# Attention and two feed-forward layers on one core: dividing P by its row sums before the transpose, V for two heads in one stationary block, and x by way of DRAM

## The chip, the cores and the metric

The kernel runs on one core of a Trainium2 chip. The metric is the device time of one execution in microseconds (us). Its engines, by the names in the profile: PE (TensorE matmuls) and PEld (TensorE weight loads), DVE (VectorE), ACT (ScalarE), POOL (GpSimd), SP (SyncE, which here only issues DMAs).

## The reference, cut to what matters

```python
q, k, v: (4, 8, 576, 64) float32          # batch, heads, tokens, head width
def _attn_ref(q, k, v, tau):
    scores = matmul(q, k.T) / sqrt(64)
    scores = where(scores >= max(scores) - tau, scores, -1e9)
    attn = exp(scores - max(scores))
    attn = attn / (sum(attn) + 1e-9)
    return matmul(attn, v)
def _moe_ref(x, w_in, w_out, g_ln):       # 2304 tokens, 512 -> 1024 -> 512
    h = x @ w_in
    solu = h * softmax(h)
    return (layer_norm(solu) * g_ln) @ w_out
def _moe2_ref(x, w_in, w_out):            # 512 -> 2048 -> 512
    h = x @ w_in
    return (h * tanh(softplus(h))) @ w_out
```

The output is _moe2_ref(_moe_ref(attention)). The weights of the two feed-forward layers (first FFN and second FFN below) arrive as float64 and are turned into float32 in the kernel.

## The kernel before

**Attention.** The 32 heads are handled as 16 pairs. For each pair, nine score tiles of 128 x 576 are made: for each of four row tiles of 128 queries one per head, and one tile that holds the last 64 queries of both heads (`s_tile`, L484). A score tile is q as stationary operand in two float32r halves (Qhh, Qb), k as moving operand (Kst), 288 columns at a time (L501). DVE takes the row maximum (L507), makes from it a bias and a threshold in one small instruction on two columns (L508), ACT computes the exponential into the SBUF tile e (L509), DVE sets to zero what lies under the threshold (L511). `turn` (L527) transposes e on PE against the identity, in blocks of 128, into the PSUM tile tp (L536, L539), and `leave` (L517) copies tp into ex, ey or er: every fourth copy on DVE (L522), the others on ACT (L523). `pv` (L562) multiplies V with the transposed tile, for each head in two pieces of 256 and 320 query columns (L575). These matmuls are float32, and the stationary block of 128 columns holds 64 columns of V and 64 of ones, so that half of the PSUM tile acc holds the product and the other half the row sums, 64 times.

**Division and x.** ACT copies the product into xT, which stays in SBUF, and the row sums into ss (L588, L589). `norm` (L595) transposes ss on DVE in 32 x 32 blocks (L598), adds 1e-9 (L600), takes the reciprocal (L601), transposes back (L602), and POOL multiplies x by it (L603). `x_split` (L614) splits x for 128 tokens into two float32r halves XH and XL on ACT and POOL.

**First FFN.** Per 128 tokens: `moe_h` (L641) makes two tiles mo of 512 columns, `layer_norm` normalizes, `moe_t` transposes (L689) and splits (L694, L696), and `moe_y` (L710) makes the output for 256 tokens in the PSUM tile smt; `moe_y` writes its two halves to DRAM. Tiles of a batch can start when its four pairs are done.

**Second FFN.** It reads these halves back and works in units of 256 or 512 tokens (L877, L903). Its buffers take the place of the attention's buffers (`opens`, L758), so it starts when the attention is over.

**Weights.** `convert` (L392) turns 128 x 256 float64 words into float32: two instructions on ACT (L404, L410), three on DVE (L412, L413, L415), one on POOL (L417).

**PSUM.** Eight banks: two score tiles st of two banks each, one each for tp, acc, mo and smt.

**What sets the order.** Every piece of work is a task with an engine, a modelled duration and its dependencies. `Plan` (L49) lists tasks with priorities from a backward pass, tries several weights, keeps the shortest list, and writes the program in that order; each engine then runs its own list strictly in that order, SP its DMA issues too. A slot of a buffer is handed on when all tasks that used it are done (L199 to L205).

Of the kernel before, what the change touches and what calls it, by code (L numbers as in the profile page):

```python
# [227 lines left out]
def kernel(  # L228
# [35 lines left out]
    NV = 2  # L264
    DV = 4
# [36 lines left out]
    w2o = [dram.tile([FG * 128, DM], F32, name=f"w2o{i}") for i in range(NG)]  # L302
    part = [dram.tile([DM, PN], F32, name=f"part{i}") for i in range(U0)]
# [158 lines left out]
    count, EXS = [0], []

    def load_v(p):

        v = VH[p % NV]
        war = [t for h in range(2) for c in range(2) for t in PVT[p - NV, h, c]] if p >= NV else []
        ld = [add("SP", dma(128 * KT * 256), lambda a=a: D(f(main(v)[:, :, 2 * a]), v2[p // (H_ // 2), p % (H_ // 2), :, a].rearrange(
            "p (k d) -> p k d", d=64)), war) for a in range(2)]
        ld.append(add("SP", dma(128 * 512), lambda: D(f(last(v)[:, 0:4:3]), v4[p // (H_ // 2), p % (H_ // 2)].rearrange("p (a d) -> p a d", d=64)), war))  # L470
        VL[p] = v, ld
# [522 lines left out]
```

## Time and profile before

| | |
|---|---|
| median of 3 runs | 1025.27 us (1023.78 to 1025.28) |
| the profiled execution | 1024.83 us; its span in the trace 1023.0 us |
| PE busy | 971.9 us (95%) |
| DVE busy | 625.7 us (61%) |
| ACT busy | 581.1 us (57%) |
| POOL busy | 302.3 us (30%) |
| chain that ended last | PE 70%, DVE 8%, ACT 7% |

A share of busy time is a mean over the whole span. The work has stretches with different limits, so the table by stretch in the rows below tells more: attention and the conversion of weights at first, then attention together with the first FFN of finished batches, then the rest of the first FFN and the second FFN. A mean duration of an instruction is from its start to its end; the next one on the same engine can start before that end.

### The profile page before, as it was taken

The numbers are of one execution on the slowest core, as the hardware profiler recorded it, in microseconds if no ns is written. First come the engines' busy times: TensorE is split into PE (matmuls) and PEld (weight loads), VectorE is DVE, ScalarE is ACT, GpSimd is POOL, SyncE is SP. The second block draws the span as 40 slices with busy tenths as digits, with TensorE's granted clock in tenths as the row PEclk, the third lists the DMA queues.
The fourth block names the chain that finished last, engine by engine and source line by source line (L and its number), as shares of the span: only waits on it lengthen the run. The fifth ranks groups of instructions, "written<-read, shape, count | busy, mean of one in ns | idle before, by whom it ended". The sixth has DMA issues, their size and how long they took to land.

```text
span 1023.0 us, 15619 instructions
## 1 busy us (share of the span) xinstructions
PE 971.9 (95%) x5648; PEld 836.8 (82%) x5648; DVE 625.7 (61%) x1309; ACT 581.1 (57%) x1166; POOL 302.3 (30%) x309
## 2 busy tenths in 40 slices
PE   3788889999999999999989999999999999999998
PEld 2676677878888898888869999998888888888887
DVE  6789989989878878778684333234544445322222
ACT  5688778988776957777674555343544234312220
POOL 3344555364432332242232110023333223200000
PEclk9799899999999999999999999999999999999999
DMA  5233324232233232231234312398645434313312
GB/s 167 75 99 93 113 70 114 69 98 91 79 99 105 75 90 68 76 93 55 68 107 141 103 44 88 107 324 283 196 138 164 152 124 144 127 59 104 124 51 72
DMA packets 106013, 113.81 MB, mean 111 GB/s; under 512 B 27472, under 2 KB 82384, under 8 KB 105936
## 3 DMA queue, kind: packets, MB, share of 16 engines
q1 hardware_dynamic: 105792, 112.82, 35.3%
q8 instruction: 44, 0.72, 0.3%
q14 instruction: 33, 0.27, 0.1%
q10 hardware_dynamic: 144, 0.00, 0.0%
HBM read 93.39 MB, written 19.40 MB: 110 GB/s over the span
## 4 chain that ended last, share of the span: by engine, by line
PE 70%; DVE 8%; ACT 7%; issue 1%; DMA 1%; ACTq 0%; SPq 0%
PE o L903 14%; PE h L877 13%; PE smt L710 8%; PE acc L575 8%; PE h2b L877 7%; PE mo L641 6%; PE o2b L903 5%; PE st L501 4%; PE tp L536 3%; ACT e L509 2%; DVE e L511 2%; DVE m L507 1%; PE mo L689 1%; DVE m L508 1%; DMA cr<-w_out 1%
## 5 line engine op out<-in xcount | busy, mean ns | idle before, releaser
L509 ACT ACTIVATE e<-st,m,sc 128x576 f32<-128x576 f32 x144 | 118.5, 830 | 41.6 <-DVE m L508 34.1
L511 DVE SCALAR_TENSOR_TENSOR e<-st,m,e 128x576 f32<-128x576 f32 x144 | 116.1, 813 | 35.5 <-ACT e L509 34.8
L417 POOL TENSOR_TENSOR cf<-cf,cl 128x256 uint32<-128x256 uint32 x96 | 71.7, 752 | 204.5 <-DVE cf L415 165.2
L501 PE MATMUL st<-Kst,Qhh 128*128 128x288 f32 (+2 forms) x352 | 111.4, 337 | 17.7 <-DVE e L511 7.6
L507 DVE TENSOR_REDUCE m<-st 128x1 f32<-128x576 f32 x144 | 107.5, 751 | 21.3 <-PE st L501 20.7
L536 PE MATMUL tp<-ident,e 128*128 128x128 f32 x576 | 92.1, 284 | 14.7 <-DVE e L511 8.6
L501 PE MATMUL st<-Kst,Qb 128*128 128x288 f32 (+2 forms) x352 | 97.8, 302 | 0.0
L536 PEld LDWEIGHTS tp<-ident,e 128*128 128x128 f32 x576 | 70.0, 145 | 32.2 <-DVE e L511 8.9
L710 PE MATMUL smt<-LH,W2H 128*128 128x256 f32 x288 | 90.9, 316 | 2.5 <-DVE yl L721 2.4
L501 PEld LDWEIGHTS st<-Kst,Qhh 128*128 128x128 f32 x352 | 70.4, 200 | 25.1 <-DVE Kst L479 7.3
L710 PE MATMUL smt<-LL,W2H 128*128 128x256 f32 x288 | 82.1, 285 | 0.0
L710 PE MATMUL smt<-LH,W2L 128*128 128x256 f32 x288 | 81.8, 284 | 0.0
L575 PE MATMUL acc<-ey,VH 128*128 128x320 f32 x256 | 79.0, 436 | 2.1 <-ACT ss L589 2.1
L501 PEld LDWEIGHTS st<-Kst,Qb 128*128 128x128 f32 x352 | 70.6, 201 | 1.7
L481 POOL TENSOR_TENSOR Qb<-Q,Qhh 128x640 fp32r<-128x640 f32 x31 | 49.1, 1585 | 76.8 <-ACT Qhh L480 72.1
L927 DVE TENSOR_TENSOR acc<-acc,o 128x512 f32<-128x512 f32 x36 | 24.7, 687 | 73.6 <-PE o L903 73.6
L575 PE MATMUL acc<-ex,VH 128*128 128x256 f32 x256 | 64.2, 385 | 2.4 <-ACT ss L589 1.3
L641 PE MATMUL mo<-W1H,XH 128*128 128x512 f32 x144 | 62.0, 430 | 0.9 <-ACT so L647 0.6
L710 PEld LDWEIGHTS smt<-LH,W2H 128*128 128x128 f32 x288 | 55.4, 192 | 6.4 <-DVE yl L721 3.4
L575 PEld LDWEIGHTS acc<-ey,VH 128*128 128x128 f32 x256 | 44.8, 190 | 17.0 <-ACT ss L589 4.0
L710 PEld LDWEIGHTS smt<-LH,W2L 128*128 128x128 f32 x288 | 55.4, 192 | 2.5
L641 PE MATMUL mo<-W1H,XL 128*128 128x512 f32 x144 | 56.7, 394 | 0.0
(157 smaller groups left out, 2689.1 us busy)
## 6 DMA issues: line engine op xcount, KB each, us to landing
y5h<-y_hi SPq DMA_DIRECT2D x26, 512.0 KB, 5.9
y5l<-y_lo SPq DMA_DIRECT2D x26, 512.0 KB, 6.8
cr<-w_in SPq DMA_DIRECT2D x48, 256.0 KB, 3.1
cr<-w_out SPq DMA_DIRECT2D x48, 256.0 KB, 2.8
Q<-qq SPq DMA_DIRECT2D x32, 320.0 KB, 2.9
K<-kk SPq DMA_DIRECT2D x32, 288.0 KB, 2.9
y2h<-y_hi SPq DMA_DIRECT2D x10, 512.0 KB, 3.9
y2l<-y_lo SPq DMA_DIRECT2D x10, 512.0 KB, 4.8
```

The costliest lines, as they stand in the source:

```text
L417: t = add("POOL", gps(CW), lambda: G.tensor_tensor(cf.tile, cf.tile, cl.tile, ALU.add), [t4, t2], use=[cl, cf])
L481: b2 = add(e, cost(SP), lambda: eng.tensor_tensor(ql.tile, q2.tile, f(qh.tile), ALU.subtract), [b], [ql], [qh, q2], port=True)
L501: TE.matmul(st.tile[:, j, c - j * HS:c - j * HS + w], q.tile[:, i * 128:(i + 1) * 128], ks.tile[:, k0:k0 + w], start=(y == x == 0), stop=( ...
L507: t = add("DVE", dve(S), lambda: V.tensor_reduce(m.tile[:, 2:3], x(), AX.XY, ALU.max, negate=True), [t], [m], [st])
L509: a = add("ACT", act(S, True) + 0.08, lambda: SC.activation(et(), x(), ACTF.Exp, bias=m.tile[:, 0:1], scale=sc), [t], [e] if h == 0 else ( ...
L511: t = add("DVE", dve(S) + 0.06, lambda: V.scalar_tensor_tensor(et(), x(), m.tile[:, 1:2], et(), ALU.is_ge, ALU.mult), [a], use=[st, e, m])
L536: TE.transpose(tp.tile[:, k * 128:(k + 1) * 128], e.tile[:, o:o + 128], ident)
L575: TE.matmul(acc.tile[:, :w], l, f(r), start=(k == 0), stop=(k == KT))
L641: TE.matmul(h.tile, l.tile[:, kt], r[:, kt, j * 512:(j + 1) * 512], start=(kt == 0 and x == 0), stop=(kt == KD - 1 and x == 2))
L710: TE.matmul(y, l[:, k, cs], r.tile[:, k], start=(k == 0 and x == 0), stop=(k == KF - 1 and x == 2))
L877: TE.matmul(h.tile[:, a * w:(a + 1) * w], l.tile[:, k, s], r.tile[:, k], start=(k == 0 and x == 0), stop=(k == KD - 1 and x == 2))
L903: TE.matmul(o.tile[:, a * w:(a + 1) * w], l.tile[:, k, ds], r.tile[:, k % n * w:(k % n + 1) * w], start=(k == 0 and x == 0), stop=(k == FG ...
```

## The change

1. The threshold instruction L516 (L511 before) sums its result into sr. The two-column op L508 becomes two one-column ops, the bias (L512) and the threshold (L515), the second not needed by the exponential.
2. `weigh` (new): 1e-9 is added to each sum (L526), a reciprocal is taken for a row tile (L527), and POOL computes (e + 0) * r in place over 576 columns, 144 times (L530). The transposes wait for POOL instead of DVE. `norm`, both DVE transposes and the multiplication of x go.
3. V of both heads is one stationary block of 128 columns. In pairs 0 to 6 (`p < F0`) the matmuls stay float32 (L586). In pairs 7 to 15 they are two float32r passes, with the high half of the transposed P and its low half (L588), against [V high, V low] of one head; ACT copies both halves of the result out (xo and tm) and POOL adds them (L605). V is split by ACT (L472) and POOL (L473).
4. `leave`: all copies out of the transposed tile on ACT (L536, L538); in pairs 7 to 15 DVE writes the low half of each (L539).
5. x goes to DRAM per pair (L607) and comes back per 128 tokens (L626). `x_split` then has one ACT and one POOL instruction.
6. PSUM: mo and smt share one tile ms of two banks, tp and acc become two slots ta; in the first four pairs every third score tile uses ms, as a third score buffer. The last two PV pieces of a pair are listed with the next pair.
7. The second head's operands, too, have their differences on DVE instead of POOL (`n < 2`).

```diff
-    NV = 2
-    DV = 4
+    F0 = 7
+    M0 = 4
...
     def load_v(p):
+        raw = lambda: q2.tile.rearrange("p (k a d) -> p k a d", a=2, d=64)
+        if p < F0:
+            v = b_v[1].new()
+            VL[p] = v, [add("SP", dma(128 * SP * 4), lambda: D(v.tile.rearrange("p k a d -> p (k a d)"), v2[p // (H_ // 2), p % (H_ // 2)]), new=[v])]
+            return
+        q2, v = b_q2.new(), b_v[0].new()
+        t = add("SP", dma(128 * SP * 4), lambda: D(q2.tile, v2[p // (H_ // 2), p % (H_ // 2)]), new=[q2])
+        hi = add("ACT", act(SP), lambda: SC.activation(v.tile[:, :, 0:4:3], raw(), ACTF.Copy), [t], [v], [q2])
+        lo = add("POOL", gps(SP), lambda: G.tensor_tensor(v.tile[:, :, 1:3], raw(), f(v.tile[:, :, 0:4:3]), ALU.subtract), [hi], use=[q2, v])
...
-        t = add("DVE", 0.08, lambda: V.scalar_tensor_tensor(m.tile[:, 0:2], ca, m.tile[:, 2:3], cb, ALU.mult, ALU.subtract), [t], use=[m], port=True)
+        t = add("DVE", 0.07, lambda: V.tensor_scalar(m.tile[:, 0:1], m.tile[:, 2:3], sc, None, ALU.mult), [t], use=[m])
...
+        t = add("DVE", 0.13, lambda: V.tensor_scalar(m.tile[:, 1:2], m.tile[:, 2:3], -1.0, t8, ALU.mult, ALU.subtract), [t], use=[m], order=[a])
         t = add("DVE", dve(S) + 0.06, lambda: V.scalar_tensor_tensor(et(), x(), m.tile[:, 1:2],
-                et(), ALU.is_ge, ALU.mult), [a], use=[st, e, m])
+                et(), ALU.is_ge, ALU.mult, accum_out=sr.tile[:, h:h + 1]), [a, t], [sr] if h == 0 else (), [st, e, m, sr], order=E[p, i][3:4])
...
+    def weigh(p, i):
+        e, sr, _, *ts = E[p, i]
+        r = lambda h: sr.tile[:, h:h + 1]
+        w = [add("DVE", 0.07, lambda h=h: V.tensor_scalar(r(h), r(h), 1.0e-9, None, ALU.add), [t], use=[sr]) for h, t in enumerate(ts)]
+        t = add("DVE", 0.08, lambda: V.reciprocal(sr.tile[:, :len(ts)], sr.tile[:, :len(ts)]), w, use=[sr])
+        for h in range(len(ts)):
+            x = lambda h=h: e.tile[:, h * S:(h + 1) * S]
+            E[p, i].append(add("POOL", 0.17 + S / 1000, lambda x=x, h=h: G.tensor_scalar(x(), x(), zero, r(h), ALU.add, ALU.mult), [t], use=[e, sr]))
...
+        t = add("ACT", act(n, True), lambda: SC.activation(dst(hi), src(), ACTF.Copy), [dep], [] if ts else [hi], [tp, hi], ts[:1])
+        x += [t, add("DVE", dve(n), lambda: V.tensor_tensor(dst(lo), src(), f(dst(hi)), ALU.subtract), [t], [] if ts else [lo], [tp, hi, lo], ts[1:2])]
...
+                for z in range(2 if p >= F0 else 1):
+                    r = u[z].tile if k == KT else x[z].tile[:, h, k] if c else x[z].tile[:, k]
+                    if p < F0:
+                        TE.matmul(acc.tile[:, :w], v.tile[:, k].rearrange("p a d -> p (a d)"), f(r), start=(k == 0), stop=(k == KT))
+                    else:
+                        TE.matmul(acc.tile[:, :w], v.tile[:, k, 2 * h:2 * h + 2].rearrange("p a d -> p (a d)"), r,
+                                  start=(k == z == 0), stop=(k == KT and z == 1))
...
+            XST[p] = add("SP", dma(128 * S * 4), lambda: D(xd[p // (H_ // 2)][k:k + 128, :], xo.tile), ts, use=[xo])
...
+            ld.append(add("SP", dma(512 * 4 * l), lambda b=b, s=s, l=l, o=o: D(
+                xr.tile[:, :, o:o + l], xd[b][:, s:s + l].rearrange("(k p) n -> p k n", p=128)),
+                [XST[p] for p in range(b * H_ // 2, (b + 1) * H_ // 2)], [] if ld else [xr], [xr], ld[:1]))
```

**How the planner's list moves.** Line numbers in rows of the change are those of the changed kernel. On DVE in the ninth pair, before; m holds maximum, bias and threshold, tt and r the row sums, LL and so belong to the first FFN:

```order
398 L660 SCALAR_TENSOR_TENSOR so,nmu<-em,se,so 128x1024
399 L511 SCALAR_TENSOR_TENSOR e<-st,m,e 128x576 x2
400 L721 TENSOR_TENSOR yl<-smt,yh 128x256
401 L662 TENSOR_SCALAR nmu<-nmu 128x1
402 L600 TENSOR_SCALAR r<-tt 128x18
403 L601 RECIPROCAL r<-r 128x18
404 L602 STREAM_TRANSPOSE tt<-r 128x576
405 L664 TENSOR_SCALAR var<-var 128x1
406 L507 TENSOR_REDUCE m<-st 128x1
407 L522 COPY ex<-tp 128x4x128
408 L508 SCALAR_TENSOR_TENSOR m<-ca,m,cb 128x2
```

and in the change, near the end of the eighth pair, the first with two passes; t_117 is the threshold constant, sr the row sums, exl, eyl, eul and evl the low halves of the transposed P:

```order
497 L516 SCALAR_TENSOR_TENSOR e,sr<-st,m,e 128x576
498 L511 TENSOR_REDUCE m<-st 128x1
499 L539 TENSOR_TENSOR eul<-ta,euh 128x128
500 L512 TENSOR_SCALAR m<-m,sc 128x1
501 L526 TENSOR_SCALAR sr<-sr 128x1 x2
502 L539 TENSOR_TENSOR eyl<-ta,eyh 128x4x128
503 L515 TENSOR_SCALAR m<-m,t_117 128x1
504 L511 TENSOR_REDUCE m<-st 128x1
505 L516 SCALAR_TENSOR_TENSOR e,sr<-st,m,e 128x576
506 L512 TENSOR_SCALAR m<-m,sc 128x1
507 L527 RECIPROCAL sr<-sr 128x2
```

The two-column op is now two, each score tile has sum ops, the block transposes are gone, and low halves stand among the score tiles.

On POOL around the operands of the fourth pair, before; cf and W1L belong to the conversion of weights, Qb and Kst to the operands of a head:

```order
41 L603 TENSOR_TENSOR xT_122<-xT_122,tt 128x576
42 L417 TENSOR_TENSOR cf<-cf,cl 128x256
43 L481 TENSOR_TENSOR Qb<-Q_787,Qhh 128x640
44 L479 TENSOR_TENSOR Kst<-K_801,Kst 64x576
45 L426 TENSOR_TENSOR W1L<-cf,W1H 128x256
46 L417 TENSOR_TENSOR cf<-cf,cl 128x256
47 L481 TENSOR_TENSOR Qb<-Q_1018,Qhh 128x640
48 L426 TENSOR_TENSOR W1L<-cf,W1H 128x256
49 L417 TENSOR_TENSOR cf<-cf,cl 128x256
```

and in the change, where e is the tile that is divided:

```order
32 L530 TENSOR_SCALAR e<-e,zero,sr 128x576 x2
33 L482 TENSOR_TENSOR Kst<-K_736,Kst 64x576
34 L530 TENSOR_SCALAR e<-e,zero,sr 128x576 x2
35 L415 TENSOR_TENSOR cf<-cf,cl 128x256 x2
36 L530 TENSOR_SCALAR e<-e,zero,sr 128x576 x2
37 L424 TENSOR_TENSOR W1L<-cf,W1H 128x256 x2
38 L484 TENSOR_TENSOR Qb<-Q_837,Qhh 128x640
39 L482 TENSOR_TENSOR Kst<-K_895,Kst 64x576
40 L415 TENSOR_TENSOR cf<-cf,cl 128x256 x2
```

The divisions stand in ones and twos between the conversions and the operands, and the multiplication of xT is gone.

On PE in the eleventh pair, before: the PV instructions of the float32 kind, one per block of V (xN counts equal ones in a row):

```order
1142 L501 MATMUL st<-Kst,Qhh 128x288
1143 L501 MATMUL st<-Kst,Qb 128x288
1144 L575 MATMUL acc<-ey,VH_151 128x320 x2
1145 L539 MATMUL tp<-ident,e 128x128
1146 L575 MATMUL acc<-ey,VH_151 128x320 x2
1147 L575 MATMUL acc<-er,VH_151 128x320
1148 L689 MATMUL mo<-ident,so 128x128 x4
1149 L536 MATMUL tp<-ident,e 128x128 x4
```

and in the change, in the tenth pair, two passes per block, into the slot ta (acc before):

```order
1019 L505 MATMUL st<-Kst,Qb 128x288
1020 L713 MATMUL ms<-LH,W2H 128x256
1021 L713 MATMUL ms<-LH,W2L 128x256
1022 L713 MATMUL ms<-LL,W2H 128x256
1023 L588 MATMUL ta<-exh,V 128x256
1024 L588 MATMUL ta<-exl,V 128x256
1025 L588 MATMUL ta<-exh,V 128x256
1026 L588 MATMUL ta<-exl,V 128x256
1027 L588 MATMUL ta<-euh,V 128x256
1028 L588 MATMUL ta<-eul,V 128x256
```

The blocks of V are passed over twice, with a high and a low half of P, in single-pass instructions, between score tiles and first-FFN matmuls as before.

## Rows read from the trace of the kernel before

**Rows 1.** from the page, its second part: TensorE's busy share in 40 equal slices of the span, in tenths.

```profile
PE   3788889999999999999989999999999999999998
```

**Rows 2.** busy times by stretch, for all instructions: the stretch, its length, then busy us (and instructions) of PE, PEld, DVE, ACT and POOL, the granted TensorE clock, the DMA share and GB/s.

```profile
0.00:207.00 207.00, 168.09 (x900) 135.27 (x901) 177.67 (x357) 158.26 (x320) 94.92 (x100) 0.95 0.34 99
207.00:515.00 308.00, 303.61 (x1919) 265.29 (x1918) 251.98 (x521) 229.29 (x464) 109.99 (x91) 1.00 0.29 83
515.00:1023.00 508.00, 500.21 (x2833) 436.26 (x2831) 196.09 (x433) 193.54 (x383) 97.36 (x119) 1.00 0.41 133
```

**Rows 3.** the same for the instructions on the score tile st alone (PE, PEld, DVE, ACT).

```profile
0.00:207.00 207.00, 61.03 (x312) 49.21 (x312) 97.44 (x127) 51.90 (x63) 0.95 0.34 99
```

**Rows 4.** waits of PE up to 207 us: engine, line waited at <- what was waited for: us in total, times, longest us.

```profile
PE tp L536 <- DVE e L511: 8.0, 3, 3.2
PE st L501 <- DVE Kst L479: 7.3, 1, 7.3
PE st L501 <- DVE e L511: 6.8, 8, 2.3
```

**Rows 5.** busy times by stretch, columns as in rows 2, for the two stretches of 50 us in which DVE is fullest beside a full PE.

```profile
150.00:200.00 50.00, 47.96 (x264) 39.00 (x265) 47.21 (x102) 43.25 (x90) 25.86 (x26) 1.00 0.33 96
200.00:250.00 50.00, 48.75 (x305) 41.37 (x303) 46.20 (x100) 42.70 (x89) 25.94 (x22) 1.00 0.31 93
```

**Rows 6.** the chain that ended last, in order of time: start us, us, engine, tile, line and instructions. Each piece lasts until the next begins.

```profile
291.42 1.62 PE acc L575 x6
...
296.64 0.86 PE acc L575 x4
...
299.25 0.53 PE st L501 x4
...
546.68 1.43 PE smt L710 x12
```

**Rows 7.** groups of instructions by line and shape: line, engine, operation, out<-in, shapes xcount | busy us, mean ns | idle us before them and what ended it. Up to 640 us, where all of each group but L412 lie.

```profile
L508 DVE SCALAR_TENSOR_TENSOR m<-ca,m,cb 128x2 f32<-128x2 f32 x144 | 51.1, 364 | 1.7
...
L412 DVE TENSOR_SCALAR cz<-cz 128x256 f32<-128x256 f32 x52 | 23.4, 452 | 1.6 <-ACT cz L410 1.4
...
L598 DVE STREAM_TRANSPOSE tt<-ss 128x576 f32<-128x576 f32 x16 | 12.3, 769 | 1.2 <-ACT ss L589 1.2
...
L600 DVE TENSOR_SCALAR r<-tt 128x18 f32<-128x18 f32 x16 | 5.9, 369 | 0.1
...
L668 DVE TENSOR_SCALAR t<-t,var 128x1 f32<-128x1 f32 x18 | 3.8, 213 | 0.6
```

**Rows 8.** the chain again, three pieces on DVE.

```profile
515.85 0.73 DVE e L511
516.58 0.08 DVE nmu L662
...
531.20 0.17 DVE t L667
```

**Rows 9.** single lines on DVE: duration in ns, least/median/most, first and last start.

```profile
L412 DVE TENSOR_SCALAR cz<-cz x96: 275/286/1653, 7.3 to 881.4; 128x256 f32<-128x256 f32 x96
L508 DVE SCALAR_TENSOR_TENSOR m<-ca,m,cb x144: 121/220/1591, 9.4 to 513.0; 128x2 f32<-128x2 f32 x144
L511 DVE SCALAR_TENSOR_TENSOR e<-st,m,e x144: 712/817/821, 10.6 to 515.8; 128x576 f32<-128x576 f32 x144
L522 DVE COPY er<-tp x24: 226/280/292, 39.9 to 522.7; 128x128 f32<-128x128 f32 x16, 64x64 f32<-64x64 f32 x8
L522 DVE COPY ey<-tp x20: 652/681/692, 30.8 to 516.6; 128x512 f32<-128x512 f32 x20
L662 DVE TENSOR_SCALAR nmu<-nmu x18: 135/144/157, 184.1 to 634.9; 128x1 f32<-128x1 f32 x18
L696 DVE TENSOR_TENSOR LL<-mo,LH x36: 652/691/693, 194.3 to 646.9; 128x512 fp32r<-128x512 f32 x36
```

**Rows 10.** instructions in order of time near 11 us: start us, us, engine, line, operation, out<-in, shapes [idle before <- what ended it].

```profile
11.29 1.54 POOL L481 TENSOR_TENSOR Qb<-Q,Qhh 128x640 fp32r<-128x640 f32 x1 [0.40 <-ACT Qhh L480]
11.36 1.62 DVE L412 TENSOR_SCALAR cz<-cz 128x256 f32<-128x256 f32 x1
```

**Rows 11.** single lines on POOL, columns as in rows 9.

```profile
L670 POOL TENSOR_SCALAR so<-so,nmu,rs x18: 1193/1198/1882, 188.5 to 638.4; 128x1024 f32<-128x1024 f32 x18
L417 POOL TENSOR_TENSOR cf<-cf,cl x96: 714/734/1058, 10.2 to 883.3; 128x256 uint32<-128x256 uint32 x96
L481 POOL TENSOR_TENSOR Qb<-Q,Qhh x31: 1529/1563/2198, 11.3 to 477.1; 128x640 fp32r<-128x640 f32 x31
L603 POOL TENSOR_TENSOR xT<-xT,tt x16: 1407/1432/2423, 86.8 to 537.6; 128x576 f32<-128x576 f32 x16
```

**Rows 12.** waits of POOL up to 207 us, columns as in rows 4.

```profile
POOL cf L417 <- DVE cf L415: 33.7, 17, 8.5
POOL Qb L481 <- ACT Qhh L480: 29.5, 11, 6.5
POOL W1L L426 <- ACT W1H L425: 22.1, 15, 3.1
```

**Rows 13.** from the page, its sixth part: a DMA issue, its count, KB of one, median us from issue to landing.

```profile
Q<-qq SPq DMA_DIRECT2D x32, 320.0 KB, 2.9
```

**Rows 14.** instructions on PE in order of time, columns as in rows 10: the one after the last PV of the attention.

```profile
537.87 0.39 PE L710 MATMUL smt<-LH,W2H 128*128 128x256 f32 x1 [2.39 <-DVE yl L721]
```

More of the change, by code (lines that the diff above doesn't have):

```diff
@@ L46, in new, with __init__ @@
         return self.slots[-1]
+class Fixed(Buf):
+    def __init__(self, part):
+        super().__init__(None, None, None, None)
+        self.part = part
+    def new(self):
+        x = super().new()
+        x.take = lambda: setattr(x, "tile", self.part)
+        return x
 class Plan:
@@ L302 @@
     w2o = [dram.tile([FG * 128, DM], F32, name=f"w2o{i}") for i in range(NG)]
+    xd = [dram.tile([DM, S], F32, name=f"xd{i}") for i in range(B)]
     part = [dram.tile([DM, PN], F32, name=f"part{i}") for i in range(U0)]
@@ L462 @@
-    count, EXS = [0], []
+    b_sr = buf("small", "sr", [128, 2], F32, 3)
+    OPS, VL, E, EX, EVT, XST = ({} for _ in range(6))
+    EXS, S3 = [], []
     def load_v(p):
[L466 to L471, printed above, removed]
+        raw = lambda: q2.tile.rearrange("p (k a d) -> p k a d", a=2, d=64)
[7 more added lines that the diff above has]
+        lo = add("POOL", gps(SP), lambda: G.tensor_tensor(v.tile[:, :, 1:3], raw(), f(v.tile[:, :, 0:4:3]), ALU.subtract), [hi], use=[q2, v])
+        VL[p] = v, [hi, lo]
@@ L476, in operands @@
                   for slot, src, w in ((k2, kk, S), (q2, qq, SP)))
-        eng, e, cost = (V, "DVE", dve) if n < 1 else (G, "POOL", gps)
+        eng, e, cost = (V, "DVE", dve) if n < 2 else (G, "POOL", gps)
         a = add("ACT", act(S), lambda: SC.activation(ks.tile, k2.tile, ACTF.Copy), [lk], [ks], [k2])
@@ L484, in s_tile @@
     def s_tile(p, i, h):
-        st, m = b_st.new(), b_m.new()
+        third = p < M0 and (9 * p + 2 * i + h) % 3 == 2
+        st, m = (b_s3 if third else b_st).new(), b_m.new()
         if h == 0:
-            E[p, i] = [b_e.new()]
-        e = E[p, i][0]
+            E[p, i] = [b_e.new(), b_sr.new()]
+        e, sr = E[p, i][:2]
         et = lambda: e.tile[:, h * S:(h + 1) * S].rearrange("p (a b) -> p a b", a=2)
@@ L592, in pv @@
-        if h and c:
-            norm(p)
-    def norm(p):
-        ss, x = EVT[p][0], xT[p // (H_ // 2) % 2][:, p % (H_ // 2)]
-        tt, r = b_tt.new(), b_r.new()
-        t = add("DVE", dve(S), lambda: V.transpose(tt.tile, ss.tile), EVT[p][1:], [tt], [ss])
-        t = chain("DVE", [
-            (0.08, lambda: V.tensor_scalar(r.tile, tt.tile.rearrange("p (a b) -> p a b", b=32)[:, :, 0], 1.0e-9, None, ALU.add)),
-            (0.18, lambda: V.reciprocal(r.tile, r.tile))], [t], [r], [tt])
-        t = add("DVE", dve(S), lambda: V.transpose(tt.tile, r.tile.unsqueeze(2).to_broadcast([128, S // 32, 32])), [t], use=[tt, r])
-        NRM[p] = add("POOL", gps(S), lambda: G.tensor_tensor(x, x, tt.tile, ALU.mult), [t], use=[tt])
+            EVT[p] = [b_xo.new(), b_tm.new() if p >= F0 else None]
@@ L750 @@
         moe_h(t, k) if kind == "h" else moe_y(t, k) if kind == "y" else moe_t(t)
-    for p, ts in EVT.items():
-        for t in ts[1::2]:
-            t.need += [(x, True) for y in XSP.values() for x in y if x.batch == p // (H_ // 2) - 2]
     W, W2Q = {}, {}
@@ L969 @@
         "v2": v2,
-        "v4": v4,
         "tau": np.full((128, 1), inputs["tau"], dtype=np.float32),
```

187 lines of the change are left out of this document (81 added, 106 removed).

## Prediction

> **What bounds the kernel now.** I began with the slices of the profile page [rows 1]: TensorE (PE) is full except at the start. The busy times by stage [rows 2] say how much; they add up to 971.9 of 1023.0 us for PE. I cut at 207 us, when 312 of the 704 score matmuls (seven pairs at 44 each) are done [rows 3], and at 515 us, after the last score tile.
>
> - Stage 1, 0 to 207 us, pairs 0 to 6: PE 168.1 us, VectorE (DVE) 177.7, ScalarE 158.3, GpSimd (POOL) 94.9. PE is idle for 39 us, and the longest of its waits are for DVE [rows 4]. DVE, at 0.858 of the stage, is the nearest to a bound.
> - Stage 2, 207 to 515 us, pairs 7 to 15 and the first FFN of the earlier batches: PE 303.6 of 308 us. PE is the bound; DVE has 252.0.
> - Stage 3, 515 to 1023 us: PE 500.2 of 508 us, nearly all second FFN, which the change leaves alone.
>
> So a us off PE counts in stages 2 and 3, and a us on DVE counts in stage 1, and in stage 2 as soon as DVE's load passes PE's. How full DVE can run beside a full PE is seen in two stretches of 50 us [rows 5]: 47.2 and 46.2 us, together 0.934, with PE at 0.967.
>
> **PE.** In the chain, four passes of a 256-column float32 matmul pair step in 0.86 us, six of 320 columns in 1.62 us, four 288-column single passes in 0.53 us, twelve of 256 in 1.43 us [rows 6]: 0.215 and 0.270 us per float32 instruction (two to a matmul), 0.133 and 0.119 us per single pass. A pair's PV is two heads x (10 x 0.215 + 10 x 0.270) = 9.7 us. In two passes it is two heads x (10 x 0.119 + 10 x 0.147) = 5.3 us; 0.147 for 320 columns is an estimate, 0.133 plus 32 columns at the slope between the two single-pass rows, rounded up. That saves 4.4 us in each of nine pairs, 39.4 us in all: 35 in stage 2, the last pair's 4.4 in stage 3. The other seven pairs keep the float32 price: one stationary block holds both heads, but each head still moves alone.
>
> The Trainium skill (TensorE: Matmul & The Clock Gate, Back-to-back issue gap) gives N/2.4 + 2.5 ns, so 109 and 136 ns for these passes, where the rows show about 0.01 us more. By the page PE would save some 4 us more; the forecast would not move, because DVE decides stage 2 in it.
>
> **DVE.** Durations overlap: a 0.82 us instruction lets the next begin after 0.73, a 0.14 us one after 0.08 [rows 8], so I take 0.08 off each mean of [rows 7] or median of [rows 9].
>
> Removed up to the last tile: the two-column bias op L508, 144 x 0.284 = 41 us; the PSUM copies L522, 36 x 0.60 + 24 x 0.19 = 26; both transposes, 32 x 0.69 = 22; L600 and the reciprocal after it, 16 x 2 x 0.29 at most, taken at 7.5. Together 96.5 us.
>
> Added: the bias multiply and the add of 1e-9, 288 one-element ops at 0.08 (0.17 if each waits for the one before, [rows 8]) = 23; the threshold op, with L668's form, 144 x 0.13 = 19; 80 reciprocals x 0.08 = 6.5; the accumulator read, 0 to 0.08, taken at 0.04 x 144 = 6; the low halves of P in nine pairs, L696's form, 9 x (9 x 0.60 + 4 x 0.20 + 2 x 0.15) = 58.5; the second head's operands 1.5. Together 114.5 us.
>
> Two corrections. DVE's two-source SBUF ops and its wide SBUF ops are held while a POOL instruction runs: L412 has a median of 0.286 and a maximum of 1.653 us, L508 0.220 and 1.591, while L511 and L696, which read PSUM, never pass 0.821 and 0.693 [rows 9]; beside a 1.54 us POOL op an L412 takes 1.62 us [rows 10]. Holding now costs the conversions about 0.17 us per L412 (mean 0.452, [rows 7]), some 15 us with the others; POOL's load grows by about 60%, so +9. And by the order seven conversions fewer come before the last tile: -7. Sum: 430 becomes 449 us. By stage: stage 1 loses 39 and gains 29, and five conversions and part of a layer norm move out, -7 more: 161. Stage 2 gets 288.
>
> If the one-element ops all took 0.17, DVE would have 26 us more; if the accumulator read were free and holding did not grow, 15 less. Both ends are in the range.
>
> **POOL.** The one-input row is L670, 1.198 us for 1024 columns; the two-input rows give a fixed part of about 0.18 us; so 576 columns take 0.75 us [rows 11], 144 of them 108 us. Also new: nine V low halves at 1.56 and nine sums at 1.43; sixteen L603 at 1.43 and one head's two differences leave. Stage 1 has 94.9 + 47 - 10 = 132 us, stage 2 about 182: covered as long as POOL's waits shrink. It is now on every tile's path: L516, +1e-9, reciprocal, POOL, transpose, some 1.5 to 2 us longer, plus POOL's queue. Stage 2 spends 308 us on 392/44 = 8.9 pairs of five row tiles, 7 us each, and three e buffers hold a row tile each: 21 us hide it.
>
> A rule speaks against this step: the Trainium skill (GPSIMD Engine Reference, Engine selection) puts elementwise work on VectorE, with one-input ops on GpSimd roughly at line rate. Followed here, 144 divisions at about 0.45 us (an estimate from L412's 0.286 for 256 columns) would put 65 us on the engine that is short, and the sum would come out about 70 us higher. The rows side with the change as long as POOL's idle time [rows 2] is usable.
>
> **Queues and transfers.** Per pair SP issues one load of V for three, plus a store of x; per token tile one load of x or two. A transfer of this size lands in about 2.9 us [rows 13]. SP's queue is in order: a store of x that waits for the last copy out of PSUM holds the Q, K and weight loads behind it. In stages 1 and 2 the token tiles of a finished batch are spread over the next batch's pairs, which hides the round trip at no cost; if it did not, a K or Q load 3 us late per pair would cost at most 16 x 3 = 48 us. At the end of attention it shows: PE waited 2.4 us for DVE there [rows 14]; in the new order 66 first-FFN output matmuls (x 0.119 = 7.9 us) stand between the last PV and the first matmul that needs the last pair's x, and the path there is two copies 0.8 + POOL 1.4 + two transfers 5.8 + a copy and a difference of 512 columns, 0.6 + 1.3 (at POOL's two-input slope): about 10. I put in 3 us. ScalarE gets L522's 60 copies and, in nine pairs, 36 copies of half sums and nine of V, and loses 64 copies of row sums: some 20 us more on 387 in the first two stages, and no bound.
>
> **Sum.** Stage 1: 161/0.858 = 188, less 3 because the third score buffer takes up part of the PE-DVE waits [rows 4]: 185. Stage 2: 288/0.934 = 308, as long as before, with PE at 0.87 instead of full; what comes off PE there is refilled by DVE. Stage 3: 508 - 4.4 + 3 = 506.5. Together 999.5 us of span against 1023.0; the profiled execution took 1024.8, 1.8 over its span (the median of the runs is 1025.3), so about **1001 us**, 2.3% faster.
>
> **Rivals.**
>
> 1. *PE stays the bound in stage 2* and DVE packs tighter than in [rows 5]: 308 - 35 = 273, total 966 us. For it: the order keeps the same 288 and 480 first-FFN matmuls before the last score matmul. Against it: DVE would need 288 of 273 us, possible only if my DVE sum is 10% too high. 0.13.
> 2. *DVE in stage 2 runs no fuller than it did in stage 1*, 0.858, because each tile's path now crosses DVE, ScalarE, POOL, PE, ScalarE, DVE: 288/0.858 = 336, total 1031 us, slower. It decides once the share falls under 0.87. For it: stage 1 is just such a mixed regime. Against: [rows 5]. 0.16.
> 3. *POOL's queue becomes the bound in stage 1.* Its waits there of 33.7, 29.5 and 22.1 us [rows 12] are for results of DVE and ScalarE; if they stay, 132 + 85 = 217 us, total 1033, slower; it decides when over 76 us of them stay. Against: in the order the divisions stand between the waiting ops, so they fill these waits. 0.08. The Trainium skill (SBUF — State Buffer, SBUF: two separate sides) calls the port that GpSimd and VectorE share an exclusive lock for a whole instruction; the trace agrees, and by that rule this rival would also lengthen DVE's conversions.
>
> The forecast keeps 0.63. A measurement of this kernel can tell about 0.2% from no change. Faster by more than that: 0.63 + 0.13 + 0.04 for milder forms of the other two = 0.80; within it 0.06; slower 0.14. Range: from rival 1 to rivals 2 and 3, 966 to 1033 us.
>
> **What would show it.** Right: the 704th score matmul still near 490 to 500 us; stage 1 about 20 us shorter; DVE over 0.9 busy in stage 2 with PE falling to about 0.87 and waiting for DVE; single passes of 0.12 to 0.15 us in PV; POOL divisions of 0.75 us; PSUM-reading DVE ops undisturbed. Wrong: PE still over 0.95 in stage 2 (rival 1), DVE and PE both under 0.88 there (rival 2), POOL over 0.8 busy with PE waiting on the divided tile (rival 3), or one-element ops stepping in 0.17 us.

## The result, and the profile after

The changed kernel takes **998.06 us** (median of 4 runs, 996.65 to 998.73), the kernel before 1025.1 beside it: a ratio of 0.9737, 95% interval 0.972 to 0.9754, so 2.6% faster. Predicted was 1001. The profiled execution took 997.51 us, its span 995.7.

The stages can be cut alike in both kernels: at the 308th score matmul (seven pairs at 44), at the last one, and at the last output matmul of the first FFN. Busy times of the kernel after, then of the kernel before at the same cuts (the cuts in [rows 2] lay 4 to 5 us later); columns as in [rows 2]:

```profile
0.00:174.50 174.50, 149.31 (x849) 123.45 (x850) 154.84 (x503) 143.79 (x297) 126.14 (x140) 1.00 0.42 125
174.50:477.80 303.30, 283.75 (x1946) 253.54 (x1945) 278.48 (x855) 247.98 (x506) 192.86 (x180) 1.00 0.32 96
477.80:638.90 161.10, 148.36 (x1070) 137.24 (x1070) 70.64 (x175) 88.28 (x175) 32.45 (x33) 1.00 0.38 121
638.90:995.70 356.80, 352.95 (x1790) 299.11 (x1788) 135.20 (x296) 114.77 (x229) 71.32 (x94) 1.00 0.45 148
```

```profile
0.00:201.90 201.90, 162.99 (x871) 130.91 (x872) 173.41 (x350) 153.38 (x310) 92.45 (x98) 0.95 0.35 101
201.90:511.20 309.30, 304.91 (x1925) 266.33 (x1923) 252.48 (x519) 230.57 (x468) 112.46 (x92) 1.00 0.28 83
511.20:664.70 153.50, 149.63 (x1058) 139.05 (x1058) 65.95 (x146) 82.27 (x160) 26.56 (x25) 0.99 0.30 98
664.70:1023.00 358.30, 354.38 (x1802) 300.53 (x1800) 133.91 (x296) 114.88 (x230) 70.79 (x94) 1.00 0.45 147
```

| stage | before | after | change | forecast |
|---|---|---|---|---|
| 1, pairs 0 to 6 | 201.9 | 174.5 | -27.4 | -22 |
| 2, pairs 7 to 15 | 309.3 | 303.3 | -6.0 | 0 |
| 3, the rest | 511.8 | 517.9 | +6.1 | -1.5 |

DVE's share is up in both first stages (from 0.859 and 0.816 to 0.887 and 0.918; forecast 0.858 and 0.934), POOL's too (to 0.72 and 0.64). The surprise is stage 3: its first 161.1 us hold no score tile and as much PE work as before (148.4 us against 149.6), yet they are 7.6 us longer. PE is full from the 3rd slice on, where [rows 1] had it full from the 7th, but the 9th, the 11th and the 20th have 8s where they had 9s:

```profile
PE   4899999989899999999889999999999999999998
...
PEclk9999999999999999999999999999999999999999
```

The granted clock is full throughout. Before, it was lower in the 2nd and the 5th slice:

```profile
PEclk9799899999999999999999999999999999999999
```

Lines of DVE and POOL that answer to [rows 9] and [rows 11] (ns: least/median/most):

```profile
L512 DVE TENSOR_SCALAR m<-m,sc x144: 192/207/216, 9.1 to 481.6; 128x1 f32<-128x1 f32 x144
...
L515 DVE TENSOR_SCALAR m<-m,t x144: 189/205/215, 9.5 to 483.5; 128x1 f32<-128x1 f32 x144
...
L526 DVE TENSOR_SCALAR sr<-sr x144: 129/145/159, 12.7 to 484.9; 128x1 f32<-128x1 f32 x144
...
L530 POOL TENSOR_SCALAR e<-e,zero,sr x144: 814/825/1775, 18.6 to 485.4; 128x576 f32<-128x576 f32 x144
...
L539 DVE TENSOR_TENSOR eyl<-ta,eyh x45: 672/684/693, 207.0 to 490.5; 128x512 fp32r<-128x512 f32 x45
```

No one-element op ever passes 216 ns, while L508, which they replace, reached 1591 [rows 9]. PSUM-reading L539 is undisturbed. In order of time, DVE shows what these ops really cost (start us, then duration):

```profile
79.95 0.08 DVE L516 DVE_READ_ACCUMULATOR e<-st,m,e 128x1 f32 x1
79.95 0.21 DVE L512 TENSOR_SCALAR m<-m,sc 128x1 f32<-128x1 f32 x1
80.07 0.20 DVE L526 TENSOR_SCALAR sr<-sr 128x1 f32<-128x1 f32 x2
80.20 0.20 DVE L515 TENSOR_SCALAR m<-m,t 128x1 f32<-128x1 f32 x1
80.32 0.15 DVE L527 RECIPROCAL sr<-sr 128x1 f32<-128x1 f32 x1
```

Each begins before the one ahead has ended: a bias or threshold op, whose scalar is read from a tile, takes 0.12 us of DVE's time, one with a constant 0.06, the accumulator read next to none (L512 begins with it).

PE in PV, where [rows 6] had 0.270 us per float32 instruction of 320 columns:

```profile
305.19 0.30 PE L588 MATMUL ta<-eyh,V 128*128 128x320 f32 x1
305.34 0.31 PE L588 MATMUL ta<-eyl,V 128*128 128x320 f32 x1
305.48 0.31 PE L588 MATMUL ta<-eyh,V 128*128 128x320 f32 x1
305.63 0.31 PE L588 MATMUL ta<-eyl,V 128*128 128x320 f32 x1
```

They step in 0.146 us; those of 256 columns in 0.120 (318.46 to 320.74 us: 19 steps in 2.28).

And PE's waits for the first FFN's matmuls, whole run, columns as in [rows 4]. Before, the longest of this kind was 2.4 us in all [rows 14]:

```profile
PE ms L713 <- ACT so L650: 7.8, 13, 0.7
PE ms L642 <- DVE yl L724: 6.2, 8, 1.4
...
PE ms L642 <- ACT yh L723: 2.5, 4, 1.5
...
PE ms L713 <- DVE yl L724: 2.3, 2, 1.2
...
PE ms L692 <- ACT yh L723: 1.5, 3, 1.1
```

L713 writes smt, the second bank of the tile ms, and waits there for a copy of the first bank (so is copied from mo); L642 and the transposes L692 write mo and wait for the readers of smt (yl, yh). Of these lines only L713 behind yl is a wait that the kernel before has too. In the chain of waits (start us, how long, what) it looks like this:

```profile
510.01 0.36 PE ms L713 x3
510.38 0.02 issue
510.40 0.61 ACT so L650
511.01 0.04 issue
511.05 0.62 PE ms L713 x3
```

### The profile page after: what moved, and what is told of

Read it like the earlier page. It is cut to its first block, busy times and chain, and to the rows that moved or that the text cites. A ratio compares the mean times of both kernels' runs of the same rounds, so it can differ in the third digit from the quotient of the medians.

```text
span 995.7 us, 16654 instructions
## 1 busy us (share of the span) xinstructions
PE 934.4 (94%) x5648; PEld 813.3 (82%) x5648; DVE 639.2 (64%) x1827; ACT 594.8 (60%) x1205; POOL 422.8 (42%) x446
## 5 line engine op out<-in xcount | busy, mean ns | idle before, releaser
L530 POOL TENSOR_SCALAR e<-e,zero,sr 128x576 f32<-128x576 f32 x144 | 122.6, 859 | 66.6 <-DVE sr L527 46.1
L513 ACT ACTIVATE e<-st,m,sc 128x576 f32<-128x576 f32 x132 | 109.8, 835 | 31.0 <-DVE m L512 23.5
L516 DVE SCALAR_TENSOR_TENSOR e<-st,m,e 128x576 f32<-128x576 f32 x132 | 107.0, 813 | 12.8 <-ACT e L513 11.2
L511 DVE TENSOR_REDUCE m<-st 128x1 f32<-128x576 f32 x132 | 98.7, 750 | 10.1 <-PE st L505 9.4
L713 PE MATMUL ms<-LH,W2H 128*128 128x256 f32 x288 | 86.1, 299 | 11.2 <-ACT so L650 7.8
L551 PE MATMUL ta<-ident,e 128*128 128x128 f32 x576 | 85.3, 277 | 8.2 <-ACT eyh L536 2.2
L551 PEld LDWEIGHTS ta<-ident,e 128*128 128x128 f32 x576 | 66.8, 141 | 20.3 <-POOL e L530 7.3
L713 PE MATMUL ms<-LL,W2H 128*128 128x256 f32 x288 | 81.2, 282 | 0.0
L713 PE MATMUL ms<-LH,W2L 128*128 128x256 f32 x288 | 81.2, 282 | 0.0
L505 PEld LDWEIGHTS st<-Kst,Qhh 128*128 128x128 f32 x312 | 60.4, 194 | 23.4 <-DVE Kst L482 10.8
L642 PE MATMUL ms<-W1H,XH 128*128 128x512 f32 x144 | 62.0, 431 | 11.2 <-DVE yl L724 6.2
L713 PEld LDWEIGHTS ms<-LH,W2H 128*128 128x128 f32 x288 | 54.5, 189 | 16.7 <-ACT so L650 11.3
L642 PE MATMUL ms<-W1H,XL 128*128 128x512 f32 x144 | 56.7, 394 | 0.0
L642 PE MATMUL ms<-W1L,XH 128*128 128x512 f32 x144 | 56.6, 393 | 0.0
```

Source lines behind the costliest of these rows:

```text
L505: TE.matmul(st.tile[:, j, c - j * HS:c - j * HS + w], q.tile[:, i * 128:(i + 1) * 128], ks.tile[:, k0:k0 + w], start=(y == x == 0), stop=( ...
L511: t = add("DVE", dve(S), lambda: V.tensor_reduce(m.tile[:, 2:3], x(), AX.XY, ALU.max, negate=True), [t], [m], [st])
L513: a = add("ACT", act(S, True) + 0.18, lambda: SC.activation(et(), x(), ACTF.Exp, bias=m.tile[:, 0:1], scale=sc), [t], [e] if h == 0 else ( ...
L516: t = add("DVE", dve(S) + 0.06, lambda: V.scalar_tensor_tensor(et(), x(), m.tile[:, 1:2], et(), ALU.is_ge, ALU.mult, accum_out=sr.tile[:, ...
L530: E[p, i].append(add("POOL", 0.17 + S / 1000, lambda x=x, h=h: G.tensor_scalar(x(), x(), zero, r(h), ALU.add, ALU.mult), [t], use=[e, sr]))
L551: TE.transpose(tp.tile[:, k * 128:(k + 1) * 128], e.tile[:, o:o + 128], ident)
```

## The experiments

My theory: DVE and the path through it set the pace in stage 1 and, once PV is in two passes, in stage 2 too (theory D). On the way I found the waits above and formed a second theory, S: they come from mo and smt being one tile. Rival to D: PE still paces stage 2 (P).

**No two-pass pairs, all two-pass pairs, no third score buffer** are one number each:

```diff
-    F0 = 7          e1: F0 = 16      e2: F0 = 0
-    M0 = 4          e3: M0 = 0
```

> All sixteen pairs keep float32 PV, the rest of the change stays. Theory D (in the changed kernel DVE and the path through it pace stage 2, PE has slack there): PE gets 34.8 us of steps back in stage 2 (320 passes, 0.2425 against 0.134 us) and 4.4 in stage 3, DVE loses 9 x 6.5 = 58.5 us; stage 1 stays 176, stage 2 is PE-bound again at about 308, stage 3 is 520: 1006, between 1002 and 1013 us. Rival P (PE still paces stage 2 after the change, so the whole PE saving is in the time): 998 + 39 = 1037 us.

> All sixteen pairs in two passes. Theory D: seven more pairs of low halves put 7 x 6.5 = 45.5 us on DVE, most of it in stage 1 where DVE is at 0.888: up to 45.5/0.888 = 51 us longer, 1049 us, at least 1030 where conversions can move out to stage 2. Rival P: PE loses 7 x 4.4 = 31 us and the time goes to 967 us.

> The score tile never uses the third buffer (M0 = 0), else the changed kernel. Forecast's term: the third buffer was worth 3 us in stage 1, so 1001 us and stage 1 at 179. Rival: it is what took stage 1 from the forecast 185 to 176: 1007 us or more. Other rival: it is worth nothing, 996 to 1000 us.

Measured: e1 1013.75 us (ratio to before 0.989, 0.9874 to 0.9907), e2 1053.3 (1.0271, 1.025 to 1.0293), e3 1004.75 (0.9804, 0.9784 to 0.9825). Stage 2 of e1, stage 1 of e2, stage 1 of e3:

```profile
175.40:496.90 321.50, 314.07 (x1962) 273.22 (x1961) 247.12 (x766) 238.23 (x488) 176.15 (x173) 1.00 0.33 100
```

```profile
0.00:203.80 203.80, 149.19 (x857) 127.91 (x858) 186.39 (x582) 156.74 (x316) 139.18 (x145) 0.89 0.34 102
```

```profile
0.00:178.60 178.60, 151.16 (x852) 124.69 (x852) 155.53 (x509) 144.99 (x299) 129.42 (x143) 1.00 0.41 126
```

P falls for this kernel: giving PE its 39 us back costs 15.7 us, not 39 (e1 lies 0.75 us over theory D's range). Without the low halves DVE is at 0.77 of stage 2 and PE at 0.98. With them everywhere, stage 1 grows by 29 us with DVE at 0.915. So two passes are worth having only where DVE has room. e2 came out 4 us over theory D's figure; its granted clock averaged 0.89 over stage 1, so a part of that stretch ran at the lower of the two levels, 1.2 GHz. How much of the 29 us is DVE's load and how much the clock was not separated. Without the third buffer the kernel is 6.7 us slower, between the two expectations. In the profiled run stage 1 is 4.1 us longer, but the first part of stage 3, where the buffer has no part, is 5.5 us longer as well: M0 changes the planner's list too, and e12 shows what that alone can do.

**Two tiles again (e4).** Once the last third score tile is read, the pool of ms is closed and two are opened. The score tiles and ta are placed from the other end of PSUM for that, which was not run alone. The edit, cut:

```diff
+    def open_m():
+        c_ms.close()
+        P["p_mo"] = pools(c1, PSUM)("p_mo")
+        smt.append(pools(c1, PSUM)("p_sm").tile([128, PN], F32, name="smt"))
+    o_m = add("-", 0.0, open_m, S3)
```

> Once the last third score tile is read, the two banks of ms become two tiles again, mo and smt; else the changed kernel. Theory S: PE's waits of first-FFN matmuls in one bank for readers of the other (18.0 us in the changed kernel: 7.8 smt for so, 6.2 and 2.5 mo for yl and yh, 1.5 transposes for yh; 9.9 of them in stage 2, 8.1 in stage 3) come from sharing one tile: all of them go. Stage 3's 8 us come off the end; stage 2's 10 may be refilled by DVE's pace: 980 to 990 us. Rival: the readers are late whatever the tile is, waits only change their name: 996 to 1000 us.

Measured: **975.04 us** (0.9513, 0.9499 to 0.9528), 23.0 us less than the changed kernel, though the list is the same, instruction for instruction, on all five engines. Stages 1 to 3a are 173.6, 292.0 and 151.2 us:

```profile
0.00:173.60 173.60, 148.66 (x850) 122.92 (x851) 154.74 (x504) 143.80 (x297) 126.21 (x140) 1.00 0.42 126
173.60:465.60 292.00, 280.44 (x1945) 253.29 (x1943) 276.88 (x855) 245.84 (x506) 192.67 (x180) 1.00 0.34 100
465.60:616.80 151.20, 146.54 (x1070) 138.72 (x1070) 71.54 (x174) 87.80 (x174) 32.70 (x33) 0.99 0.40 129
```

Its chain at the place shown above has no copy between the matmuls any more:

```profile
495.64 2.75 PE mo L642 x12
498.39 0.71 PE smt L713 x6
499.10 1.43 PE h L890 x12
```

S holds: all four kinds of wait are gone. The time is 5 us under its range, since more than the 18.0 us of shown waits went. A matmul's record lasts 0.28 us where its step is 0.12, so a wait shows about 0.16 us too short. In the changed kernel (start us, duration, idle before it):

```profile
510.08 0.28 PE L713 MATMUL ms<-LL,W2H 128*128 128x256 f32 x1
511.05 0.39 PE L713 MATMUL ms<-LH,W2H 128*128 128x256 f32 x1 [0.69 <-ACT so L650]
```

The trace says 0.69, but 0.97 us lie between the two starts, and the step takes 0.12 of them. With 28 such waits that is 4.5 us more, an estimate of 22.5 us in all. Two waits that the program needs grew by 2.1 us (for yl from 2.3 to 3.4, for LL from 1.1 to 2.1), so some 20 of the 23.0 us measured are accounted for. Stage 2's part was not refilled; DVE went from 0.918 to 0.948 there. In this program the waits follow the tile: with two tiles the same matmuls and copies go on side by side.

**The division on DVE (e5)**, one multiplication in place per tile (the line is cut):

```diff
-            ... add("POOL", 0.17 + S / 1000, ... G.tensor_scalar(x(), x(), zero, r(h), ALU.add, ALU.mult), ...
+            ... add("DVE", dve2(S), ... V.tensor_scalar(x(), x(), r(h), None, ALU.mult), ... port=True))
```

> The changed kernel with the division on DVE, one multiplication of 576 columns by r in place, instead of on POOL. Theory D: 144 of them at 0.37 us a step (the 0.45 of the prediction less the overlap of 0.08) put 53 us on DVE, 23 in stage 1 and 30 in stage 2; POOL loses 123 of 423 us, and the conversions on DVE that it holds win back 10 to 15. About 40 us more DVE work at a share of 0.9: 998 + 44 = 1042, between 1030 and 1065 us. Rival: POOL's longer path (0.86 us and its queue) cost as much as the DVE work would, 995 to 1010 us.

Measured: 1036.12 us (1.0109, 1.0092 to 1.0127), 38 us over the changed kernel. DVE's load in stages 1 and 2 rises from 433.3 to 485.7 us, its shares to 0.923 and 0.953:

```profile
L530 DVE TENSOR_SCALAR e<-e,sr x144: 499/511/1812, 22.6 to 523.7; 128x576 f32<-128x576 f32 x144
```

```profile
0.00:189.80 189.80, 157.17 (x856) 129.94 (x857) 175.22 (x549) 144.06 (x288) 76.14 (x76) 0.98 0.36 112
189.80:515.60 325.80, 293.72 (x1948) 258.80 (x1947) 310.51 (x942) 250.24 (x510) 122.75 (x98) 0.98 0.28 86
```

Theory D's range holds: 52.4 us more work on DVE cost 38.1 us at the end, 0.73 us for each. The list is another one, and POOL lost 116 us of work.

**The joint op back (e6, e9).** In e6 the bias and the threshold are one two-column op again, and the planner makes a new list. In e9 the list of the changed kernel is kept on the other four engines; on DVE the joint op stands where the bias op stood. The two constants ca and cb are set once at the start. Of the edit only the operations:

```diff
-    V.tensor_scalar(m.tile[:, 0:1], m.tile[:, 2:3], sc, None, ALU.mult)
+    V.scalar_tensor_tensor(m.tile[:, 0:2], ca, m.tile[:, 2:3], cb, ALU.mult, ALU.subtract)
-    V.tensor_scalar(m.tile[:, 1:2], m.tile[:, 2:3], -1.0, t8, ALU.mult, ALU.subtract)
```

> The changed kernel with the two-column op for bias and threshold back, which DVE shares with POOL's instructions, instead of two ops on one column. Theory H (held while POOL runs): its mean was 0.364 us before and is 0.45 or more beside POOL's 423 us; DVE has 142 x (0.37 - 0.245) = 18 us more, and the exponential waits for a held op: 1012 to 1030 us. Rival: two ops that step in 0.125 and 0.12 us cost as much as one that steps in 0.14 with little holding, 993 to 1002 us.

> The changed kernel with its list kept word for word on TensorE, ScalarE, GpSimd and SyncE; on DVE the two-column op stands where the bias op stood, and nothing where the threshold op stood. Theory H: the op is held by POOL's instructions and the exponential waits for it, so most of the 28 us that the joint op cost in a list of its own come back: 1010 to 1028 us. Rival L: those 28 us were the other list, and in this list the two forms cost the same: 996 to 1003 us.

Measured: e6 1025.95 us (1.0005, 0.9993 to 1.0018), e9 1021.22 (0.9962, 0.9949 to 0.9974), both in theory H's range; rival L falls. With the joint op the whole change is worth nothing or 0.4%. L517 of e9 is the joint op, first all of them, then those up to the last score tile (busy us, mean ns), then stages 1 and 2:

```profile
L517 DVE SCALAR_TENSOR_TENSOR m<-ca,m,cb x144: 196/231/1547, 9.4 to 505.4; 128x2 f32<-128x2 f32 x144
```

```profile
L517 DVE SCALAR_TENSOR_TENSOR m<-ca,m,cb 128x2 f32<-128x2 f32 x142 | 69.3, 490 | 0.8
```

```profile
0.00:183.90 183.90, 152.90 (x850) 124.33 (x851) 162.09 (x445) 144.85 (x297) 125.56 (x140) 0.99 0.39 118
183.90:501.50 317.60, 289.58 (x1946) 256.11 (x1945) 290.98 (x775) 248.35 (x506) 192.10 (x180) 0.99 0.30 92
```

Its mean went from 0.364 us before [rows 7] to 0.490, its maximum is 1.547, and the exponential's waits for it rose from 23.5 us to 43.6. In DVE's time, an estimate with the overlap of 0.08: 142 x (0.490 - 0.08 - 0.245) = 23.4 us, as much as the kernel lost (23.2). One such case in e9 (start us, duration), where the joint op ends with the POOL instruction beside it:

```profile
61.67 1.56 POOL L489 TENSOR_TENSOR Qb<-Q,Qhh 128x640 fp32r<-128x640 f32 x1
61.74 1.51 DVE L517 SCALAR_TENSOR_TENSOR m<-ca,m,cb 128x2 f32<-128x2 f32 x1
```

The divisions themselves do little of the holding. The 29 joint ops of e9 that begin while POOL runs a division last 0.358 us on average, the 29 that begin beside a difference for Qb or Kst 0.965, and the 52 that begin beside no POOL instruction 0.212. Of the 39 us that all 144 last beyond 0.216 us each, 4 lie beside the divisions and 22 beside Qb and Kst.

The Trainium skill (SBUF — State Buffer, SBUF: two separate sides) says why it is this op and not its successors: a DVE op with two SBUF inputs takes part in the lock with a GpSimd op that reads SBUF, and the loser waits for the whole instruction. The runs agree: the two-input op lasts up to 1.547 us, the one-input ops of one column never beyond 0.216.

**Less work on DVE (e7, e8, e10, e11)**, all on e4's kernel. e7 leaves out the addition of 1e-9 and lets the planner make a new list; e10 keeps e4's list less these 144 ops. e8 and e11 multiply the factor 1/8 into q instead of the bias, with one more POOL instruction per head; e8 with a new list, e11 with e4's and without the 1e-9 as well.

```diff
-    w = [add("DVE", 0.07, lambda h=h: V.tensor_scalar(r(h), r(h), 1.0e-9, None, ALU.add), [t], use=[sr]) ...]       e7
+    w = [add("DVE", 0.07, lambda: None, [t], use=[sr]) ...]                                                         e10
-    V.tensor_scalar(m.tile[:, 0:1], m.tile[:, 2:3], sc, None, ALU.mult)                                             e8, e11
+    G.tensor_scalar(q2.tile, q2.tile, zero, sc, ALU.add, ALU.mult)
```

> Two tiles as in the run before it, and 1e-9 is not added to the row sums (a row's maximum contributes exp(0) = 1 to its sum). Theory D (DVE at 0.95 in stage 2 paces it): 142 ops that step in 0.06 us are 8.5 us off DVE, so 975 - 9 = 966, between 963 and 969 us. Rival: such a small op fits into gaps, 973 to 976 us.

> Two tiles, and the factor 1/8 is multiplied into both halves of q (by ACT's copy, and by one more POOL instruction of 640 columns per head), so that the exponential's bias is the negated maximum itself and the op for it goes. Theory D: 142 ops that step in 0.125 us are 17.8 us off DVE, and the exponential starts 0.13 us sooner: 975 - 19 = 956, between 952 and 962 us. Rival: POOL's 32 x 0.92 = 29 us more lie on the operands' path or hold DVE's conversions: 968 to 980 us.

> The kernel with two tiles, its list kept word for word, less the 144 ops that add 1e-9. Theory D: DVE paces both first stages, 142 x 0.06 = 8.5 us go: 964 to 970 us. Rival G: they fit into gaps that stay: 973 to 976 us. Third: slower than 976 us, then something other than the list made the same edit slower with a list of its own.

> The kernel with two tiles, its list kept, without the 1e-9 ops and without the bias ops: the factor 1/8 goes into both halves of q, by ACT's copy and by one more instruction of 640 columns per head (on POOL, for the first two heads too) right ahead of the difference. Theory D: 8.5 + 17.8 = 26 us off DVE, and the exponential comes 0.13 us sooner: 948 to 956 us. Rival: 32 more POOL instructions of 0.9 us delay operands or divisions: 960 to 980 us.

**The same work in another list (e12)**, e4 with one planner cost at 0.08 for 0.07:

> The same work as the kernel with two tiles, but the planner's cost for the 1e-9 op is 0.08 instead of 0.07, which gives another list. Theory L (lists of the same work differ by as much as the edits): 5 to 12 us away from 975. Rival: 973 to 977 us, and then what the no-1e-9 kernel lost with a list of its own is not the list's luck.

Measured: e7 981.96 us (0.9583, 0.9566 to 0.9599), e8 1001.46 (0.9766, 0.9748 to 0.9783), e10 **973.66** (0.9502, 0.9483 to 0.9522), e11 982.35 (0.9591, 0.9569 to 0.9614), e12 979.28 (0.9557, 0.9538 to 0.9576). Theory D's figures failed in all four. e10 falls in rival G's range; e7, e8 and e11 are slower than their rivals' ranges too. e12 lies just under what theory L asked. Stage 2 of e10, and PE's longest waits in e11 apart from the first loads:

```profile
173.10:465.00 291.90, 280.64 (x1947) 253.62 (x1946) 273.96 (x776) 246.12 (x506) 192.95 (x180) 1.00 0.33 100
```

```profile
PE ta L556 <- POOL e L535: 6.2, 6, 1.2
PE st L510 <- POOL Kst L487: 3.9, 6, 1.3
```

Two things follow. First, lists of the same work differ: e12 is 4.2 us behind e4, and the edit of e7 is 8.3 us worse in a list of its own than in e4's. Differences under some 10 us between kernels with different lists (e3's among them) say little of the edit, and e1's 15.7 us hold an unknown part of that kind. Second, in e4's list theory D is only half true: e10 takes 5.3 us of busy time off DVE in stage 1 and 2.9 in stage 2, and gets 0.5 and 0.1 us there. PE is at 0.96 and DVE at 0.94 of stage 2, so with the false waits gone neither has much to give alone. e11 also moves the load to POOL, and PE then waits for POOL's results (6.2 and 3.9 us), the way its rival said. What slowed e8 stays open; its stage 1 is shorter than e4's (167.8 us), its stage 2 longer (320.7 us). The lowest time is e10's, 5.0% faster than before and 2.4% faster than the change; e4's is 1.4 us more, and the intervals of the two overlap.

## Why the prediction was right, and where it was not

- **Stage 1 is bound by DVE:** right in one direction. Work put on it moves the end (e5, e9, and e2 in stage 1, there beside a lower clock). Work taken off it hardly does: 5.3 us less gave 0.5 us (e10, beside two tiles, with DVE and PE both at 0.86 of the stage). The sum went from the forecast 161 to 154.8 us, the share from 0.858 to 0.887.
- **The clock of stage 1:** the prediction put nothing on it. Before, the granted clock averaged 0.95 over that stage, so parts of it ran at the lower of the two levels, 1.2 GHz; PE was busy for 7 and 8 tenths of the two slices with the low clock [rows 1]. After, it is 1.00, and PE's busy time there fell from 163.0 to 149.3 us for 871 and 849 instructions. As an estimate, 0.05 x 201.9 = 10 us of PE's time came back. How many of the stage's 27.4 us that is, no run separates.
- **PE's saving:** right to the hundredth: 0.120 and 0.146 us a pass for the forecast 0.119 and 0.147. The formula that the prediction quotes from the Trainium skill (TensorE: Matmul & The Clock Gate, Back-to-back issue gap) is given there for an isolated matmul, which no run here times, while these passes follow one another.
- **"What comes off PE there is refilled by DVE":** right in kind. Two passes save PE 39 us and the kernel 15.7 (e1). Rival 1, the 966 us with PE still the bound, is refuted for the change as it ran. But PE read 0.935 in stage 2, not the 0.87 that was to be the sign: records of 0.28 us cover the gaps between steps of 0.12. Without the false waits PE reads 0.960 there (e4), over the 0.95 that was to be rival 1's sign, and DVE work taken off gives 0.1 us (e10); which engine paces that stage then is not shown. The last score matmul came at 477.8 us, ahead of the 490 to 500.
- **DVE's sum in attention:** forecast 449, measured 433.3 us. The bias op was dearer (0.125 for 0.08), the threshold op 0.12 for 0.13, the add 0.06 for 0.08, the accumulator read next to nothing for 0.04, and a conversion's three ops rose from 1.20 to 1.33 us, which is +5 over 41 of them for the +9. The 16 us too many were worth 6.2/0.858 + 9.5/0.934 = 17 us of the forecast.
- **The joint op, L508:** taken as -41 and, for what replaces it, +30.5. By the measured steps against the kernel before it is 144 x (0.284 - 0.245) = 5.6 us. But with POOL 40% busier over the run, keeping it would have cost 23 us more than splitting it (e9), so the split is worth 23 of the change's 27 us. That the divisions need it is not shown: the ops beside them are held little. The prediction named the holding and put its price on the conversions alone.
- **POOL:** 0.859 us a division for 0.75 (median 0.825), which did not matter: POOL is at 0.72 of stage 1, and its waits there have shrunk from 33.7, 29.5 and 22.1 us [rows 12] to 18.9 and less, so rival 3 is refuted:

```profile
POOL e L530 <- DVE sr L527: 18.9, 3, 18.2
POOL cf L415 <- DVE cf L413: 5.8, 7, 1.7
```

- **The division's engine:** the Trainium skill (GPSIMD Engine Reference, Engine selection) would have it on VectorE; that is 38 us slower here (e5). The prediction said 70: DVE's load grew by 52 us, not 65, and its shares rose with it.
- **The step that failed: the shared PSUM tile.** The prediction costed point 6 of the change at -3 us in stage 1 and nothing elsewhere. One tile for mo and smt made the matmuls into either bank wait for the readers of the other: 22.2 us of span (995.7 against 973.5, e4), 11.3 of it in stage 2, 9.9 in the first part of stage 3. That hid how well the rest works: without it the change gives 4.9%.
- **The end of attention:** the +3 us for the longer handover fit by subtraction alone. Free of the false waits, the first part of stage 3 is 151.2 us against 153.5: -4.4 for the last PV leaves +2.1.
- **Rival 2** (a share of 0.858 in stage 2): refuted, 0.918 and, without the false waits, 0.948.

So 1001 against 998 is closer than the working deserves, and that is luck: two errors of over 20 us cancel. The DVE sum was 17 us too dear. Its shares without the false waits came out higher than forecast, worth 4 us in each of the first two stages (154.7/0.858 - 3 = 177.4 against 173.6; 276.9/0.934 = 296.5 against 292.0). Against these 25 us stand 22 us of false waits: 999.5 - 25 + 22 is 996.5, and the span was 995.7.

## What to carry to other kernels

When a change puts two PSUM buffers into one tile, price it as a dependency: every writer of one half may now wait for the readers of the other, and such waits show too short where matmul records overlap. When GpSimd gets busier, look at which small ops on VectorE take two SBUF inputs, above all one that another engine waits for, and which GpSimd instructions they meet; splitting such an op into one-input ops may be worth more than the move itself. Where a planner sets the order, test an edit in the same list, since a new list alone moves the time by several us.

## What was not expected of the hardware

- A one-column DVE op whose scalar is read from a tile steps in 0.12 us, one with a constant in 0.06; the accumulator read after the threshold op costs next to nothing.
- A two-column op on DVE can last as long as the POOL instruction beside it: 1.51 us beside 1.56 (e9).
- A division of 576 columns on DVE is held by POOL as well: least 0.499, most 1.812 us, and all 16 that take over 0.7 us overlap a POOL instruction (e5).
- TensorE's busy share hides waits: in stage 2 of the changed kernel it reads 0.935, and 11 us of a stage of 303 could still be had without touching its work.
